# Mask of the first tile added to the scores on TensorE, scheduler priorities by batch, and a last output tile in two column halves, in an attention and gated-MLP kernel

One core of one Trainium2 chip. The metric is the time of one execution in microseconds (us) on the device. Unless it says otherwise, a position is in us from the start of the profiled span, which is some 2 us shorter than the time of the execution.

## The reference

```python
# q, k, v: (4 batches, 8 heads, 768 positions, 64) float32; block = 32; 24 blocks
scores = np.matmul(q, k.transpose(0, 1, 3, 2)) / np.sqrt(64)
mask = (abs(blk_i - blk_j) <= 1) | (first and last block, rows and columns)
mask |= (3 sampled blocks in each block row)
scores = np.where(mask, scores, -1e9)
attn = softmax(scores) ;  x = (attn @ v) as (3072 tokens, 512)
h = x @ w_in                      # w_in: 512 x 2048
out = (h / (1 + np.exp(-beta * h))) @ w_out        # w_out: 2048 x 512
```

## The kernel before

Scores are made transposed (keys on partitions), two heads together, each on 64 rows of the array. ACT takes the exponential of 1024 scores a partition, DVE multiplies it by a 0/1 mask, PE multiplies by the values with one column of ones for the sum, and DVE divides. Four such head pairs give a tile of tokens (256 or 512). For it PE makes 16 hidden pieces, ACT a tanh of each (the gate is written with tanh), DVE the product, PE the output, ACT or DVE the copy, and a DMA stores it.

```python
            def mm(sc=sc, kc0=kc0):
                kX, qX = at(kq)
                for i in range(kn):
                    for hh in range(2):
                        pe.matmul(
                            at(sc)[:, hh, i * n:(i + 1) * n],
                            lhsT=kX[hh * D:(hh + 1) * D, (kc0 + i) * P:(kc0 + i + 1) * P],
                            rhs=qX[hh * D:(hh + 1) * D, q0:q0 + n].rearrange(
                                "d (g c p) -> d c g p", c=CG, p=P),
                            start=True, stop=True)
            def ex(eng, sc=sc, et=et):
                act.activation(out=..., in_=..., func=AF.Exp, bias=0.0, scale=SCALE)
            def mk(eng, et=et, kc0=kc0):
                ...
                dve.tensor_tensor(out=e, in0=e, in1=m, op=ALU.mult)
```

The order of instructions on each engine is made ahead by a list scheduler in the kernel's own Python. All pieces of work are nodes with durations and dependencies. At each step it takes the node with the smallest sum of earliest start and a priority of its kind; the priorities are fitted numbers.

```python
                bias = BIAS[n.kind]
                ...
                key = (n_start + n.dur[e] - min(n.dur.values()) + bias, n.place)
                if best is None or key < best[0]:
                    best = (key, n, e, n_start)
```

The weights come by the DMA queue of POOL in four parts (two of w_in, two of w_out), the first held back until a certain k tile has landed; q, k, v by the queue of SP.

The softmax here doesn't subtract the row's maximum and nothing guards it: scores larger than these inputs give would overflow.

## Time and profile before

| before | |
|---|---|
| time, median (this and its later runs) | 277.1 us (276.2 to 279.0 over all later runs) |
| profiled span | 275.0 us |
| first exponential | 6.86 |
| first hidden matmul of the first (256 wide) tile | 30.18 |
| first hidden matmul of the second (512 wide) tile, "the boundary" | 61.12 |
| last matmul's end, and the tail after it | 270.7, and 4.2 us |

The table is a skeleton of the span: a ramp up to the boundary, a body in which PE has no break, and a tail. The lines behind it are in the prediction. All spans and milestones below are from one profiled execution of each kernel; ratios are from several runs.

### The profile page before, as it was taken

The numbers are of one execution on the slowest core, as the hardware profiler recorded it, in microseconds if no ns is written. First come the engines' busy times: TensorE is split into PE (matmuls) and PEld (weight loads), VectorE is DVE, ScalarE is ACT, GpSimd is POOL, SyncE is SP. The second block draws the span as 40 slices with busy tenths as digits, with TensorE's granted clock in tenths as the row PEclk, the third lists the DMA queues.
The fourth block names the chain that finished last, engine by engine and source line by source line (L and its number), as shares of the span: only waits on it lengthen the run. The fifth ranks groups of instructions, "written<-read, shape, count | busy, mean of one in ns | idle before, by whom it ended". The sixth has DMA issues, their size and how long they took to land.

```text
span 275.0 us, 6172 instructions
## 1 busy us (share of the span) xinstructions
PE 259.7 (94%) x2455; PEld 139.7 (51%) x2455; DVE 209.2 (76%) x416; ACT 217.1 (79%) x284; POOL 32.5 (12%) x53
## 2 busy tenths in 40 slices
PE   6677899969999999999999999999999999999993
PEld 2454674544455464455464444444545644567441
DVE  4789999998797798798988787977787877628000
ACT  3799998998789988789988788987798977529110
POOL 7243000043200112110010111030000000000000
PEclk9999999999999999999999999999999999999999
DMA  6999995599521798796577529490121300020222
GB/s 178 295 267 213 207 205 143 150 265 210 145 49 49 194 165 225 169 220 139 174 190 172 112 61 258 88 224 8 55 62 54 44 12 0 13 86 2 77 76 77
DMA packets 72882, 36.66 MB, mean 133 GB/s; under 512 B 29828, under 2 KB 68756, under 8 KB 72852
## 3 DMA queue, kind: packets, MB, share of 16 engines
q1 hardware_dynamic: 69600, 32.06, 47.3%
q0 software_dynamic: 3136, 4.19, 8.6%
q8 instruction: 19, 0.31, 0.5%
q14 instruction: 11, 0.09, 0.1%
q10 hardware_dynamic: 116, 0.01, 0.0%
HBM read 27.27 MB, written 6.29 MB: 122 GB/s over the span
## 4 chain that ended last, share of the span: by engine, by line
PE 88%; DVE 5%; ACT 2%; DMA 2%; SPq 1%; issue 1%; ACTq 0%; DVEq 0%
PE sc L208 88%; DVE et L208 2%; ACT et L208 2%; DMA st_k<-in_k_dram 2%; DVE xst L208 1%; SPq L477 1%; DVE recip L208 0%; DVE kX L208 0%; DVE s_k L208 0%; DVE xT_sb L208 0%; ACT qX L208 0%; ACT osb L208 0%; SPq L474 0%; DVE s_q L208 0%; DVE qX L208 0%
## 5 line engine op out<-in xcount | busy, mean ns | idle before, releaser
L208 ACT ACTIVATE et<-sc 128x1024 f16<-128x1024 f32 x144 | 136.4, 1045 | 13.9 <-PE sc L208 13.4
L208 DVE TENSOR_TENSOR et<-et,mask 128x1024 f16<-128x1024 f16 x144 | 94.8, 693 | 8.1 <-ACT et L208 8.0
L208 PE MATMUL sc<-w_out_sb,g 128*128 128x512 f16 x384 | 90.0, 379 | 0.0
L208 PE MATMUL sc<-xT_sb,w_in_sb 128*128 128x512 f16 (+1 forms) x448 | 84.3, 349 | 1.1 <-DVE xT_sb L208 1.0
L208 ACT ACTIVATE t_sb<-sc,beta_h_sb 128x512 f16<-128x512 f32 (+1 forms) x112 | 68.2, 649 | 17.1 <-PE sc L208 17.1
L208 DVE SCALAR_TENSOR_TENSOR g<-t_sb,sc 128x512 f16<-128x512 f16 (+1 forms) x112 | 67.6, 611 | 16.0 <-ACT t_sb L208 15.6
L208 PEld LDWEIGHTS <-w_in_sb 128*128 128x128 f16 x448 | 43.8, 98 | 40.7 <-issue 1.5
L208 PEld LDWEIGHTS <-g 128*128 128x128 f16 x384 | 34.6, 98 | 43.2 <-issue 7.5
L208 PE MATMUL sc<-qX,kX 64*128 64x256 f16 (+1 forms) x384 | 44.0, 339 | 4.7 <-ACT qX L208 1.9
L208 PEld LDWEIGHTS <-et 128*128 128x128 f16 x1152 | 39.7, 98 | 9.7 <-issue 6.6
L208 PE MATMUL sc<-va,et 128*128 128x65 f16 x1152 | 42.4, 194 | 1.1 <-ACT et L208 1.0
L208 PEld LDWEIGHTS <-kX 64*128 64x128 f16 x384 | 16.4, 98 | 26.5 <-issue 19.2
L208 ACT ACTIVATE osb<-sc 128x512 f32<-128x512 f32 x18 | 11.0, 608 | 17.9 <-PE sc L208 17.9
L208 DVE TENSOR_TENSOR xst<-sc,recip 128x256 f16<-128x256 f32 x48 | 20.3, 424 | 1.8 <-DVE recip L208 0.2
L497 POOL CAST s_k<-st_k 128x768 f16<-128x768 f32 (+1 forms) x11 | 8.2, 753 | 76.7 <-DMA st_k<-in_k_dram 76.6
L208 DVE RECIPROCAL recip<-sc 128x4 f32<-128x4 f32 x48 | 8.7, 180 | 10.4 <-PE sc L208 8.7
L497 POOL CAST s_q<-st_q 128x768 f16<-128x768 f32 (+2 forms) x11 | 9.0, 821 | 33.4 <-DMA st_q<-in_q_dram 33.0
L497 POOL CAST va<-st_v 128x768 f16<-128x768 f32 x7 | 6.6, 939 | 19.7 <-PE sc L208 15.2
L208 DVE CAST va<-st_v 128x768 f16<-128x768 f32 x9 | 5.0, 558 | 0.9 <-DMA st_v<-in_v_dram 0.9
L208 PE MATMUL sc<-identity,s_k 128*128 128x128 f16 x24 | 3.5, 305 | 2.0 <-DVE s_k L208 1.2
L208 DVE CAST s_k<-st_k 128x768 f16<-128x768 f32 x7 | 3.9, 554 | 1.4 <-issue 0.7
L208 DVE COPY xT_sb<-sc 128x256 f16<-128x256 f16 (+1 forms) x9 | 3.1, 346 | 1.8 <-PE sc L208 1.8
(53 smaller groups left out, 44.6 us busy)
## 6 DMA issues: line engine op xcount, KB each, us to landing
st_v<-in_v_dram SPq DMA_DIRECT2D x16, 384.0 KB, 5.1
out_dram<-osb SPq DMA_DIRECT2D x24, 256.0 KB, 2.2
st_k<-in_k_dram SPq DMA_DIRECT2D x15, 384.0 KB, 4.8
st_q<-in_q_dram SPq DMA_DIRECT2D x12, 384.0 KB, 4.2
w_in_sb<-in_moe_w_in_dram POOLq DMA_DIRECT2D x2, 1024.0 KB, 9.9
w_out_sb<-in_moe_w_out_dram POOLq DMA_DIRECT2D x2, 1024.0 KB, 16.6
st_q<-in_q_dram SPq DMA_DIRECT2D x12, 128.0 KB, 4.6
st_k<-in_k_dram SPq DMA_DIRECT2D x3, 128.0 KB, 2.6
```

The costliest lines, as they stand in the source:

```text
L208: r = f(*a, **kw)
L477: nc.sync.dma_start(out=o[:, g::NG], in_=hg[:, g::NG])
L497: e(out=at(dst)[:, :, :, 0:D] if nm == "v" else by_chunk(dst, lo, hi), in_=src)
```

## The change

The intent: take 12 mask multiplies off DVE in the ramp by adding -30000 to the closed scores on PE before the exponential (two more matmuls of the one-hot block pattern in front of each score pair of the first tile); give each batch its own priorities; let the last output tile end in a shorter copy and store; and let the scheduler's model know that the loading queue has eight lanes. The buffers were newly divided as well.

```diff
-BIAS = {"av": -69, "beta": -455, "cast": 94, "dma": -1239, "ex": 257, "gm": -727, "hp": -468,
+BIAS = {"av": (-653, -382, -588, -2130),
+        "beta": (141, 4011, -951, 12518),
... (25 entries, four numbers each)
+ORDER = "k0a q0 k0b k0c v0 k1 q1 v1 k2 q2 v2 k3 q3 v3 r0 r1 r2 r3"
+N_PEMASK = 4
+GATES = ("k3", None, None, None)
...
+                if e == "SP":
+                    for i in range(n.lanes):
+                        n_start = max(n_start, lane[(n_lane + i) % 8])
-                bias = BIAS[n.kind]
+                bias = BIAS[n.kind][n.part]
...
-                wire[other] += both / RATE[other]
+                wire[other] += both / RATE[e]
...
-    SLOTS = {"st_k": 2, "st_q": 5, "st_v": 5, "s16_k": 4, "s16_q": 2, "set": 4, "va": 4,
-             "et": 13, "xst": 5, "recip": 7, "t_sb": 6, "g": 2, "osb": 3, "sc": 4}
+    SLOTS = {"st_k": 2, "st_q": 3, "st_v": 2, "s16_k": 3, "s16_q": 2, "set": 7, "va": 5,
+             "et": 17, "xst": 6, "recip": 30, "t_sb": 4, "g": 2, "osb": 2, "sc": 4}
... (in the score step)
+                        if by_pe:
+                            r = slice(hh * D, (hh + 1) * D)
+                            pe.matmul(
+                                at(sc)[:, hh, i * n:(i + 1) * n],
+                                lhsT=onehot[r, (kc0 + i) // CG, :],
+                                rhs=shut_qk[r, ...],
+                                start=True, stop=False)
...
-                            start=True, stop=True)
+                            start=not by_pe, stop=True)
... (in the output step)
+            end = t0 + ts * P + P == N_TOK
+            w = D_MODEL // 2 if end else D_MODEL
+            for m0 in range(0, D_MODEL, w):
... (matmuls, copy and store of w columns each)
```

## The prediction

> **What bounds the kernel now.** I read the page from the top: who is busy, and when.
>
> ```profile
> PE 259.7 (94%) x2455; PEld 139.7 (51%) x2455; DVE 209.2 (76%) x416; ACT 217.1 (79%) x284; POOL 32.5 (12%) x53
> PE   6677899969999999999999999999999999999993
> ACT  3799998998789988789988788987798977529110
> ```
>
> PE is the engine, but not in all of the span: the slices (6.9 us each) show it short of 9 in the first five, in the ninth and in the last. The table of stretches (columns: stretch, length, then busy us of PE, PEld, DVE, ACT, POOL, then clock, DMA share, GB/s) says who is full there.
>
> ```profile
> 5.00:10.00 5.00, 3.71 (x30) 2.14 (x29) 2.54 (x7) 3.87 (x6) 2.02 (x5) 1.00 1.05 295
> 20.00:25.00 5.00, 3.62 (x47) 1.83 (x46) 4.73 (x10) 5.00 (x7) 2.76 (x4) 1.00 1.13 215
> 25.00:30.00 5.00, 4.20 (x66) 2.59 (x64) 4.33 (x12) 5.00 (x6) 0.00 (x0) 1.00 1.13 208
> 55.00:60.00 5.00, 3.28 (x66) 2.36 (x63) 4.93 (x11) 5.00 (x6) 1.88 (x3) 1.00 0.96 255
> 150.00:200.00 50.00, 50.00 (x413) 23.93 (x412) 40.77 (x72) 42.20 (x55) 5.96 (x7) 1.00 0.49 119
> ```
>
> From 20 to 60 us ACT is full and DVE nearly; from 61 us on PE is full and ACT has a sixth of its time free. So there are two regimes: to 61 us the exponentials on ACT set the pace, after it PE does. The busy share hides how slow PE is at first; the timeline shows it with equal bundles of 12 score matmuls:
>
> ```profile
> 10.92 1.46 PE L208 MATMUL sc<-qX,kX 64*128 64x256 f16 x12 [0.96 <-ACT qX L208]
> 17.95 0.83 PE L208 MATMUL sc<-qX,kX 64*128 64x256 f16 x12 [0.92 <-ACT qX L208]
> 61.12 5.12 PE L208 MATMUL sc<-xT_sb,w_in_sb 128*128 128x512 f16 x23 [0.58 <-DVE xT_sb L208]
> ```
>
> The last line is the boundary: the first hidden-layer matmul of the second token tile (512 wide). From there to the end the chain of waits has PE in one unbroken piece:
>
> ```profile
> 60.65 0.43 DVE xT_sb L208
> 61.12 209.62 PE sc L208 x1870
> 270.81 0.60 ACT osb L208
> ```
>
> To turn this into a ledger I took the start-to-start distance of matmuls of one kind in the warm part of the trace: 216 ns for 512 columns, 109 for 256, 32 for a value matmul (65 columns), 56 for a transpose; a score pair (two heads, different rows of the array) 216 or 110 together. Times the counts this gives 239.7 us of work, 35.3 below the span. By stretch the difference is 17.8 us in 0 to 30, 1.1 in 30 to 50, 3.4 in 50 to 60, 4.2 in the tail after the last matmul, and some 8 in 61 to 270. The order of instructions has 76 changes between 64-row and 128-row matmuls in that last stretch, so 105 ns a change explains those 8 us.
>
> **What the Trainium skill says.** "TensorE: Matmul & The Clock Gate", Part 1: PE starts at half clock until it has been busy through a whole window of about 3.4 us, 107 against 56 ns for 128 columns. The trace agrees: transposes early are 107 ns apart (median), later ones 56, and the two bundles above are 1.46 and 0.83 us. The same page, Part 3, The mechanism: matmuls on different row groups run together, starting about 4 ns apart. Here the second head starts 3 to 4 ns after the first. The mask matmuls are such pairs, so 48 of them cost 24 single ones. "ScalarE: Activation LUTs", What ACT_TABLE_LOAD costs: 186 ns + 0.833 per element, with 93 ns overlapped back to back; for 1024 elements an estimate of 946 ns. The trace has 144 exponentials in 136.4 us, 947 each. "DMA: Bandwidth & Descriptors", Anatomy of one DMA: some 2 us are fixed per transfer. The output stores land 2.2 us after issue at 256 KB, so halving one can't halve its tail.
>
> **The change, part by part.**
>
> Mask on PE, first tile only. It takes 12 mask multiplies off DVE: 12 x 0.69 = 8.3 us (group of et<-et,mask, 693 ns), in 9 to 19 us. It adds 48 matmuls of 256 columns in 24 pairs: 24 x 0.11 = 2.6 us warm, 24 x 0.24 = 5.8 us cold (12 in 1.46 us). It also takes DVE out of the path from exponential to values, and lets the values of head pair 3, whose exponentials were done by about 21.5 us but whose values ran only at 27.15, run earlier. Its price at the start: a PSUM-to-SBUF ACTIVATE of 384 columns (estimate 0.5 us between the 0.37 of 256 columns and the 0.65 of 512) now sits on ACT before the first exponential, and cold mask pairs precede the first scores. The first exponential, at 6.86 us, I put at 7.4.
>
> Priorities. The order of the two builds shows what they do. ACT reaches its first 512-wide tanh after 41 exponentials instead of 45, and the first 256-wide tanh after 18 instead of 23: less attention ahead, hidden layer earlier. Hidden work costs PE far more per ACT time (a 512-wide hidden step: 4 x 216 ns of PE for one 0.69 us tanh, and as much PE again for the output layer) than attention (216 ns of scores and 8 x 32 of values for 947 ns), so this moves PE's full regime forward. I add up ACT between its first exponential and its first 512-wide tanh:
> - before: 45 x 0.947 = 42.6; 16 narrow tanh x 0.41 = 6.6; 2 output copies 1.2; one token copy 0.6; three narrow and one wide q copy 1.8: 52.8 us. The stretch is 62.19 - 6.86 = 55.3, so 2.5 us are gaps.
> - after: 41 x 0.947 = 38.8; tanh 6.6; output copies 1.2; one 768-wide k copy (estimate 0.9) and one q copy 0.4: 47.9 us, plus the same 2.5 of gaps.
> So the first wide tanh comes at 7.4 + 50.4 = 57.8 instead of 62.2, and the first wide hidden matmul, 1.1 us ahead of it as now, at 56.7 instead of 61.1: 4.4 us gained.
>
> The weights allow it, just. Both halves of w_in land 9.9 us after issue (15.37 and 20.25), at 25.3 and 30.1 us; before, the hidden layer starts at 30.18, so only the second half was used on arrival. The new order runs the first 32 hidden matmuls, scores, then the rest, which fits the two arrivals. The two halves of w_out release their waiters at 35.3 and 40.9, and the new order meets them with output pieces of 4 matmuls with attention between.
>
> After the boundary. PE's remaining work by the same costs is 202.4 us against 201.7, with 78 row changes against 76: 0.9 us given back. ACT is tighter in the first wide hidden tile and what follows: between the first wide matmul and that of the next tile it gets 31 exponentials, 16 wide tanh (0.69) and 3 output copies, 42 us, and PE some 43.5. ACT is 97% full there against 89% before (26 exponentials); I charge 0.5 us for waits.
>
> Last output tile in halves. The last ACT copy has 256 columns instead of 512: 0.60 to an estimated 0.38. The store has 128 KB instead of 256: perhaps 0.3 us less of the 2.2. Matmul time stays (32 x 109 against 16 x 216). Sum 0.5 us.
>
> DMA lanes in the model. They cost nothing on the chip; they make the planned order of loads closer to what the queue does. Fewer staging buffers (q 5 to 3, v 5 to 2) pay for more exponential buffers (13 to 17). I give it 0.
>
> Sum: 275.0 - 4.4 + 0.9 + 0.5 - 0.5 = 271.5 us of span, 3.5 less. On the median of 277.07 that is 273.6. I take 273.0: the gaps (2.5 us) are probably smaller in the new order too, since DVE has 8.3 us less to do exactly where they lie (ACT waited there for copies of q and k that stood behind mask multiplies), and the author tuned for that.
>
> **Rivals.** (1) The ramp gives nothing: cold mask matmuls delay the second head pair's scores, since in the new PE order the values of the first pair stand ahead of them. If those 24 matmuls run cold (1.53 us, as at 13.19 now) ACT idles up to 2 us near 11. For it: the 1.46 us bundles. Against it: PE is busy without break from 5 us on, so its clock may rise sooner. It would make 275. (2) ACT stays the bound beyond the boundary because it has less done ahead, 41 exponentials against 45, and the gain is handed back in 57 to 100 us. For it: 97%. Against it: by the second wide tile 72 exponentials are done against 71. It would make 275 to 276. (3) Loads arrive late with fewer staging buffers, and PE waits in the middle. For it: the load queue already stood from 41.9 to 52.2 us behind stores and transposes. Against it: PE has no loss at all in 65 to 250 beyond row changes. It would make 274 to 278. (4) The clock rises early and DVE's relief closes the gaps: the boundary moves to 54 to 55 us and the time to 271.
>
> **Range and chances.** The sum rests on one large term, 4.4 us, uncertain by some 2 us each way (start of the first exponential, gaps), and on no new stall later. So 273.0, with 270.2 to 275.7 for 8 in 10. Faster by over 2% needs less than 271.5, which takes rival 4: 0.28. Slower by over 2% would need a broken prefetch: 0.03.
>
> **What would show it.** Right: the first wide hidden matmul at 55.5 to 58 us; the stretch 55 to 60 with PE near 5.0; first exponential at 7.2 to 7.7; the first narrow hidden matmul near 25.5 (w_in) rather than 30.2; PE unbroken after the boundary, some 214 us from it to the end; the last ACT copy near 0.38 us. Wrong: ACT gaps of over 1 us near 11, PE waits for et or DMA after 60, or a boundary still at 60.

## The result, and the profile after

| | before | after |
|---|---|---|
| time, median of 4 runs | 277.11 us (276.81 to 277.69) | 272.70 us (272.37 to 273.64) |
| profiled span | 275.0 | 270.5 |
| first exponential | 6.86 | 7.17 |
| values of the fourth head pair | 27.15 | 21.67 |
| first narrow hidden matmul | 30.18 | 25.37 |
| the boundary | 61.12 | 55.88 |
| last matmul's end | 270.73 | 266.97 |
| tail | 4.22 | 3.50 |

The ratio is 0.9844, with a 95% interval of 0.9815 to 0.9873. A ratio here is the mean time of one kernel's fast runs over that of the other's of the same rounds, so not quite the ratio of the medians.

From the page of the kernel after, the engines' busy us with their shares, and PE and ACT in 40 slices:

```profile
PE 260.1 (96%) x2519; PEld 141.5 (52%) x2519; DVE 194.1 (72%) x397; ACT 216.8 (80%) x289; POOL 37.3 (14%) x58
PE   6988999999999999999999999999999999999994
ACT  4898999799988989979978878987898788695111
```

Besides the first slice and the last, PE is short of 9 in slices 3 and 4 only, where it was so in 2 to 5 and in 9. DVE has 15 us less to do: 7.4 of them are mask multiplies, and six output copies (4.1) have gone to ACT, some casts to POOL. The stretches of the kernel after (same columns as in the prediction):

```profile
5.00:10.00 5.00, 4.76 (x44) 3.05 (x44) 2.18 (x6) 4.11 (x8) 2.13 (x4) 1.00 1.12 305
20.00:25.00 5.00, 4.04 (x68) 2.36 (x65) 3.85 (x11) 3.88 (x6) 1.12 (x2) 1.00 1.14 219
25.00:30.00 5.00, 4.52 (x41) 3.52 (x41) 4.84 (x14) 5.00 (x12) 0.00 (x0) 1.00 1.12 210
55.00:60.00 5.00, 4.54 (x27) 1.85 (x26) 4.77 (x7) 4.98 (x7) 3.62 (x4) 1.00 1.34 309
150.00:200.00 50.00, 50.00 (x413) 23.93 (x411) 36.95 (x66) 42.54 (x55) 6.35 (x8) 1.00 0.46 116
```

The stretch 55 to 60, in which PE had 3.28 us of 5, is now 4.54: the body has moved into it. ACT has given back time in 20 to 25 (3.88 for 5.00). It is a wait of 1.12 us for scores whose second half of q came late. The timeline (start, length, engine, line, operation, tiles and shapes, then the idle time ahead and who ended it) around the start of the hidden layer and around the boundary:

```profile
25.34 0.35 PEld L244 LDWEIGHTS <-w_in_sb 128*128 128x128 f16 x4 [0.64 <-DMA w_in_sb<-in_moe_w_in_dram]
25.37 0.60 PE L244 MATMUL sc<-xT_sb,w_in_sb 128*128 128x256 f16 x4 [0.50 <-DVE xT_sb L244]
31.06 1.05 PE L244 MATMUL sc<-xT_sb,w_in_sb 128*128 128x256 f16 x8 [0.29 <-DMA w_in_sb<-in_moe_w_in_dram]
55.88 3.63 PE L244 MATMUL sc<-xT_sb,w_in_sb 128*128 128x512 f16 x16
59.97 2.32 PE L244 MATMUL sc<-xT_sb,w_in_sb 128*128 128x512 f16 x10 [0.46 <-DVE g L244]
```

The first narrow hidden matmul waits for two things at once: its weights (PEld is released by the landing of w_in's first half) and its tokens (PE is released by DVE's copy of xT_sb). Before, only the second bound:

```profile
30.18 4.00 PE L208 MATMUL sc<-xT_sb,w_in_sb 128*128 128x256 f16 x33 [0.45 <-DVE xT_sb L208]
```

The chain of waits of the kernel after (start, length, what) now begins with another part of the same load, the second half of w_in, which landed at 31.01 and for which PE waited 0.29 us:

```profile
18.58 12.43 DMA w_in_sb<-in_moe_w_in_dram
31.06 3.55 PE sc L244 x32
...
59.97 207.02 PE sc L244 x1882
267.00 0.38 ACT osb L244
```

Its last piece of PE has no break for 207 us, as before (209.6), and the copy behind it takes 0.38 us, not 0.60. So the 4.5 us of span are -5.2 at the boundary, +1.5 from there to the last matmul (211.1 for 209.6), and -0.7 in the tail.

### The profile page after: what moved, and what is told of

Its sections match the earlier page's. It is cut to its first block, busy times and chain, and to the rows that moved or that the text cites. A ratio compares the mean times of both kernels' runs of the same rounds, so it can differ in the third digit from the quotient of the medians.

```text
span 270.5 us, 6288 instructions
## 1 busy us (share of the span) xinstructions
PE 260.1 (96%) x2519; PEld 141.5 (52%) x2519; DVE 194.1 (72%) x397; ACT 216.8 (80%) x289; POOL 37.3 (14%) x58
## 4 chain that ended last, share of the span: by engine, by line
PE 82%; DMA 5%; DVE 3%; ACT 2%; issue 0%
PE sc L244 82%; DMA w_in_sb<-in_moe_w_in_dram 5%; DVE et L244 2%; ACT et L244 2%; DVE xT_sb L244 0%; DVE g L244 0%; DVE xst L244 0%; ACT osb L244 0%; DVE recip L244 0%
## 5 line engine op out<-in xcount | busy, mean ns | idle before, releaser
L244 DVE TENSOR_TENSOR et<-et,mask 128x1024 f16<-128x1024 f16 x132 | 87.4, 704 | 6.4 <-ACT et L244 6.2
L244 PE MATMUL sc<-w_out_sb,g 128*128 128x512 f16 (+1 forms) x400 | 90.3, 371 | 0.0
L244 PE MATMUL sc<-xT_sb,w_in_sb 128*128 128x512 f16 (+1 forms) x448 | 86.8, 349 | 1.3 <-DVE xT_sb L244 0.5
L244 DVE SCALAR_TENSOR_TENSOR g<-t_sb,sc 128x512 f16<-128x512 f16 (+1 forms) x112 | 64.4, 607 | 15.7 <-ACT t_sb L244 15.4
L244 ACT ACTIVATE t_sb<-sc,beta_h_sb 128x512 f16<-128x512 f32 (+1 forms) x112 | 66.0, 637 | 11.7 <-PE sc L244 7.3
L244 ACT ACTIVATE osb<-sc 128x512 f32<-128x512 f32 (+1 forms) x25 | 14.8, 590 | 19.4 <-PE sc L244 18.7
L565 POOL CAST va<-st_v 128x768 f16<-128x768 f32 x12 | 10.5, 873 | 64.9 <-DMA st_v<-in_v_dram 64.1
L565 POOL CAST s_q<-st_q 128x768 f16<-128x768 f32 (+1 forms) x11 | 8.9, 811 | 12.0 <-DVE g L244 5.4
L244 PE MATMUL sc<-shut_qk,onehot 64*128 64x256 f16 x48 | 6.8, 306 | 0.4 <-ACT et L244 0.4
L244 DVE CAST s_q<-st_q 128x512 f16<-128x512 f32 (+2 forms) x9 | 3.7, 407 | 1.5 <-DMA st_q<-in_q_dram 1.5
```

Source lines behind the costliest of these rows:

```text
L244: r = f(*a, **kw)
L565: e(out=at(dst)[:, :, :, 0:D] if nm == "v" else by_chunk(dst, lo, hi), in_=src)
```

## The experiments

All twelve kernels give the right result. They ran in four groups, each on one chip and beside runs of the kernel before on it: e1, e2, e6, e7; then e3, e4, e5, e9; then e0, e12, e13 (five rounds each); then e14 (three rounds). Two ways of ablation are used, and the difference turned out to matter: some rerun the scheduler on a changed input, so that the whole order moves; some keep the order of the changed kernel and alter one thing in it. Where the profile of a kernel is quoted, it is of one execution.

### The last tile

**e1**: before, with the output step of the change (two halves in the last tile). Apart from the last tile the order is that of before.

```diff
+            end = t0 + ts * P + P == N_TOK
+            w = D_MODEL // 2 if end else D_MODEL
+            for m0 in range(0, D_MODEL, w):
```

> The kernel before with only the last output tile in two halves; all other instructions keep their order. My theory: only the end changes. The last output copy takes 0.38 us instead of 0.60 and the last store ends sooner, so the span falls by 0.5 to 0.8 us, from 275.0 to about 274.3 (ratio 0.997 to 0.998). Rival, the fixed part of a store hides it: only the copy's 0.22 us show, span 274.8 (0.999). Either way the first wide hidden matmul stays at 61.1 us.

**e2**: the changed kernel with its last tile whole.

```diff
-            w = D_MODEL // 2 if end else D_MODEL
+            w = D_MODEL
```

> The changed kernel with its last output tile whole again; nothing else moves. My theory: the halves are worth the 0.74 us by which the stretch from the last matmul to the end is shorter (4.27 against 3.53 us), so the span becomes 271.0 to 271.3 and the ratio to before 0.987. Rival, the halves are worth nothing: 270.5, ratio 0.984.

**e12**: the changed kernel with the last tile cut at 384 and 128 columns.

```diff
-            for m0 in range(0, D_MODEL, w):
+            for m0, w in ((0, 384), (384, 128)) if end else ((0, D_MODEL),):
```

> The changed kernel with its last output tile cut at 384 and 128 columns instead of 256 and 256. Theory (after the last matmul only the last part's copy and store remain): the last copy falls from 0.38 to about 0.28 us and its store of 64 KB lands some 0.1 us sooner, tail 3.3 to 3.4 us against 3.53, so 0.1 to 0.3 us less in all, ratio 0.983 to 0.986, within the spread of the times. Rival: the first part's larger store (192 KB), issued shortly before, keeps the queue, and the tail is 3.5 or more.

Measured: e1 0.9979 [0.9942, 1.0017], 276.46 us; e2 0.9844 [0.9803, 0.9884], 273.16 us (0.987 was expected); e12 0.9837 [0.9802, 0.9872], 272.32 us. The last copies in the timelines of e1 and of e12:

```profile
271.26 0.38 ACT L208 ACTIVATE osb<-sc 128x256 f32<-128x256 f32 x1 [1.31 <-PE sc L208]
```

```profile
266.61 0.49 ACT L244 ACTIVATE osb<-sc 128x384 f32<-128x384 f32 x1 [2.00 <-PE sc L244]
267.45 0.28 ACT L244 ACTIVATE osb<-sc 128x128 f32<-128x128 f32 x1 [0.36 <-PE sc L244]
```

From last matmul to end of span: 4.2 us before, 3.5 in e1 and after, 4.0 in e2, 3.1 in e12 (the expectation of e2 has 4.27 and 3.53, from rounded spans). In the traces the halves are worth 0.5 to 0.7 us, and the cut at 384 another 0.4, a little more than I had expected. In the times none of it is resolved: the interval of e1 includes 1, and e2 has the changed kernel's ratio. The times of one kernel differ by more than 1 us between runs; where from is the last experiments' subject.

### The mask on PE, with the order kept

**e6**: the changed kernel's order on ACT, SP, POOL and PE; the mask matmuls are taken out, and 12 mask multiplies go into DVE's order behind their exponentials.

```diff
-                        if by_pe:
+                        if False:
...
-                            start=not by_pe, stop=True)
+                            start=True, stop=True)
+    for e, f, et in late:                 # after the scheduler has run
+        n = Node("mk", "DVE", 0, 0, f)
+        seq.insert(first_after(e, et), n)
```

> The changed kernel in its own order on PE, ACT, SP and POOL, but without the mask matmuls: the 12 masks of the first tile are multiplied on DVE again, each at the first place in DVE's queue at which its exponential is planned to be done. My theory: the order lives off DVE's relief. DVE is busy 5.9 of 10 us in 10 to 20 us, 8.3 us more do not fit without delay, and the values of the first tile wait for their masks: first narrow hidden matmul 1 to 4 us later than 25.4, first wide one at 57 to 60 instead of 55.9, ratio 0.988 to 0.996. Rival, the order alone makes the gain and the mask matmuls only cost PE 2.6 us and the first exponential 0.4 us: same as the changed kernel or faster, ratio 0.980 to 0.985.

**e7**: the mask matmuls doubled (the closed scores get -60000, with the same result).

```diff
+                            for again in range(2):
                               pe.matmul(
...
-                                start=True, stop=False)
+                                start=again == 0, stop=False)
```

> The changed kernel with each mask matmul issued twice (48 more, in 24 pairs, at the same places). My theory: they lie beside ACT, which sets the pace of the first tile, so most of the 2.6 to 5 us added to PE is hidden; the first exponential comes 0.4 us later (two more cold pairs ahead of it) and the time grows by 0.4 to 1.2 us, ratio 0.986 to 0.989. Rival, PE is on the path there: 3 us or more longer, ratio 0.995 or above.

Measured: e6 0.9908 [0.9879, 0.9937], 274.75 us; e7 0.9903 [0.9873, 0.9932], 274.68 us. DVE (third busy column) in 15 to 25 us, first in the kernel after, then in e6:

```profile
15.00:20.00 5.00, 3.86 (x71) 2.88 (x66) 2.87 (x10) 5.00 (x6) 3.11 (x4) 1.00 1.10 233
20.00:25.00 5.00, 4.04 (x68) 2.36 (x65) 3.85 (x11) 3.88 (x6) 1.12 (x2) 1.00 1.14 219
```

```profile
15.00:20.00 5.00, 3.24 (x56) 2.32 (x56) 5.00 (x12) 4.15 (x6) 4.52 (x5) 1.00 1.19 258
20.00:25.00 5.00, 3.74 (x69) 2.55 (x66) 5.00 (x13) 4.46 (x6) 0.00 (x0) 1.00 1.12 210
```

With the multiplies DVE is full for those 10 us, and everything that stands behind it is late: the tokens of the first tile (first hidden matmul at 27.57 for 25.37) and with them the boundary (57.62 for 55.88). The two places in e6:

```profile
27.57 0.60 PE L244 MATMUL sc<-xT_sb,w_in_sb 128*128 128x256 f16 x4 [0.91 <-DVE xT_sb L244]
57.62 3.63 PE L244 MATMUL sc<-xT_sb,w_in_sb 128*128 128x512 f16 x16
```

PE waits in 15 to 30 us for DVE's copies of q, k and the tokens. So in this order the mask on PE is worth 1.7 us at the boundary, and the times agree (e6's median is 1.6 us above that of e2, the same order but for the last tile, in the same rounds). The other 3.5 of the 5.2 us come with the order itself, its new buffers included (61.12 to 57.62, e6 having no mask on PE). Not separated from DVE's relief is the clock: the trace's first record of a full clock is at 9.5 us in the kernel after, 14.6 in e6 and 16.6 before. In the ten profiles with the mask on PE it comes at 8.5 to 14.4 us, in the four without at 14.6 to 19.3.

e7 costs more than I had expected for 24 pairs: the first exponential is 0.62 us later, the first hidden matmul 1.11, the boundary 0.80, but the next wide tile 2.1 us later (102.17 for 100.08). The second loss is at the boundary itself. Timelines there, after and then e7:

```profile
55.58 3.74 DVE L244 TENSOR_TENSOR et<-et,mask 128x1024 f16<-128x1024 f16 x4
56.21 1.34 POOL L565 CAST va<-st_v 128x768 f16<-128x768 f32 x1 [0.50 <-DMA st_v<-in_v_dram]
```

```profile
56.37 5.04 DVE L244 TENSOR_TENSOR et<-et,mask 128x1024 f16<-128x1024 f16 x4
58.79 0.85 POOL L565 CAST va<-st_v 128x768 f16<-128x768 f32 x1 [0.37 <-DMA st_v<-in_v_dram]
```

Four multiplies take 5.04 us in e7, 3.74 after, and 2.5 at their usual 0.62 from one to the next; POOL casts run beside them: three in the kernel after (up to 1.34 us, 0.83 alone), five in e7 (0.83 to 1.07). The Trainium skill, "SBUF — State Buffer", Who interferes with whom, says that a VectorE instruction with two SBUF inputs contends with a GpSimd instruction that reads SBUF. The direction fits both traces. No run isolates it, and casts and multiplies overlap in the records, so I claim no more than that this place is sensitive to when POOL's casts fall.

### The parts, with the scheduler run again

**e3**: the change without the mask on PE. **e4**: the change with the priorities of before. **e5**: before, with the mask on PE alone. **e9**: the change with the second part of q of the first head pair loaded one place earlier, meant to close ACT's gap of 1.12 us.

```diff
-N_PEMASK = 4                                   # e3
+N_PEMASK = 0
+BIAS = {"av": -69, ... of before}              # e4
+BIAS = {k: (v,) * 4 for k, v in BIAS.items()}
+N_PEMASK = 4                                   # e5, in before, with the code of the mask matmuls
-ORDER = "... k3 q3 v3 r0 r1 r2 r3"             # e9
+ORDER = "... k3 q3 r0 v3 r1 r2 r3"
```

> The changed kernel with no tile masked on PE; the scheduler is free to make another order (36 exponentials before the first wide tanh and 23 before the first narrow one, 45 between the first wide hidden matmul and that of the next tile). My theory: the mask on PE is what lets these priorities pay. The first narrow hidden matmul comes at 28 to 31 us as in the kernel before, and ACT has 45 exponentials and 16 wide tanh, 54 us, to do in the first wide hidden tile, for which PE needs 48, so that PE waits there. Ratio 0.989 to 0.999. Rival, the priorities make the gain alone: 0.985 or less.

> The changed kernel with the priorities of before, the same in each batch. The order has 43 exponentials before the first wide tanh instead of 41, 19 before the first narrow one, and three token copies on ACT. By my ledger that is 2 x 0.95 + 3 x 0.4 = 3 us more on ACT before the boundary, which lies at 58 to 60 us: ratio 0.992 to 0.998. Rival, the mask on PE makes the gain and the priorities none: 0.984 to 0.987.

> The kernel before with the mask of the first tile on PE and nothing else (its priorities, buffers and loads). The order has 18 exponentials before the first narrow tanh instead of 23, but still 45 before the first wide one. My theory: the boundary is set by ACT's sum, which is that of before plus 0.5 us for making the mask operand: first narrow hidden matmul at 25 to 27 us, first wide one still at 60 to 62, ratio 0.997 to 1.004. Rival, DVE's relief alone shortens the ramp: boundary at 57 to 58, ratio 0.986 to 0.990.

> The changed kernel with the second part of the first q loaded before the last v of the first four pairs. In the changed kernel ACT waits 1.12 us near 20 us for scores that need this q (landed at 18.6). My theory: the gap closes, but the new order puts 42 exponentials before the first wide tanh instead of 41, so the two cancel: ratio 0.982 to 0.987. Rival, the gap was on the path and nothing comes back: 0.980 or less.

| | ratio and interval | median | first hidden | boundary | next wide tile |
|---|---|---|---|---|---|
| e3 | 1.0900 [1.0862, 1.0939] | 302.42 | 37.34 | 68.57 | 130.26 |
| e4 | 0.9986 [0.9967, 1.0005] | 277.23 | 27.40 | 60.50 | 101.92 |
| e5 (one slow run left out) | 1.0182 [1.0149, 1.0215] | 282.22 | 27.64 | 62.37 | 108.78 |
| e9 | 1.0419 [1.0379, 1.0460] | 288.85 | 25.57 | 58.87 | 105.91 |

Three of four missed what I had expected, by 1.4% (e5) to 9% (e3), and e4 missed narrowly. None is the change less one part. In each the scheduler makes another order, and with priorities fitted to another problem it makes a poor one. In e3 PE waits 4.4 us for a q cast in 20 to 36 (from the waits of PE, in total, times, longest), its clock is halved for most of 30 to 40 (seventh number), and PE is idle after the boundary too; e9 has such a wait at 140 to 180. The lines, e3 twice, then e9:

```profile
PE sc L244 <- DVE s_q L244: 4.4, 1, 4.4
30.00:40.00 10.00, 6.83 (x52) 4.35 (x53) 7.58 (x18) 3.90 (x7) 1.34 (x2) 0.51 0.92 161
```

```profile
PE sc L244 <- DVE va L244: 3.4, 1, 3.4
```

What follows: the parts don't add up. Everything but the new priorities gives nothing (e4), the mask alone costs 1.8% under the old ones (e5), and the new ones without the mask cost 9% (e3). I conclude that the gain belongs to the order that was fitted for exactly this program; which of its features make the 3.5 us no run isolates. A build without a run belongs here: with the lane term alone taken out of the scheduler's model, the program comes out identical on all five engines. So that term by itself does nothing in this kernel.

### The early clock, and the spread of the times

e2 is the changed kernel up to its last tile, and yet its first 24 value matmuls took longer in the trace than those of the kernel after, the second line here, by the half clock of PE:

```profile
10.72 1.53 PE L244 MATMUL sc<-va,et 128*128 128x65 f16 x24
```

```profile
9.68 1.20 PE L244 MATMUL sc<-va,et 128*128 128x65 f16 x24
```

Its score matmuls ran at half rate until 14.4 us. I took this for the source of the spread, and ran the changed kernel again (**e0**, no edit) beside a version whose early idle time is filled (**e13**).

> The changed kernel, unaltered, to have its spread and its early clock beside the next two. Expected 0.984 to 0.987 of the time before, medians 272.4 to 273.4. My theory of the ramp (the same program gets its full clock at 9 to 11 us in some runs and near 14 in others) says that single times spread over at least 1.5 us and that the profiled run shows the first bundle of 24 values either near 1.2 us or near 1.5. The rival (the late clock in the run with a whole last tile came from that kernel, not from chance) says spread below 0.8 us and the bundle near 1.2 again.

```diff
+                if lo == 0 and (x, nm) in ((0, "q"), (1, "k")):
+                    for _ in range(4 if x else 3):
+                        pe.matmul(at(tb)[:, 0:256 if x else 128], lhsT=warm[:, 0:P],
+                                  rhs=warm[:, 0:256 if x else 128], start=True, stop=True)
```

> The changed kernel with seven dummy matmuls more (three of 128 columns before the first q transposes, four of 256 before the k transposes of the second head pair), placed where PE waits in its first 11 us; the order is otherwise the same. If it is PE's idle time there that delays the clock, the profile shows the value bundle near 1.2 us or less, the boundary at or below 56.0, the single times spread less than those of the unaltered kernel, and the ratio is 0.980 to 0.984. If the phase of the clock is set by something else than PE's work, the dummies only stand in the way: boundary 56 to 57, ratio 0.984 to 0.988, spread as before.

Measured: e0 0.9861 [0.9829, 0.9893], 273.10 us (272.45 to 274.47); e13 0.9862 [0.9819, 0.9905], 273.35 us (271.75 to 276.41, of which the highest is a slow run and left out of the ratio). The boundary of e13 is as expected (55.57), but the value bundle took 1.33 us where 1.2 or less was expected, since the full clock came at 11.4 us, later than in the kernel after (9.5); and its times are neither better nor closer together. And the profile of e0 contradicts me: its values ran early and fast (9.60, 0.99 us), its thirteenth exponential was the earliest of all (20.85), and its boundary was the latest, 57.39. The time was lost later. Timeline and stretches of e0:

```profile
25.68 0.61 PE L244 MATMUL sc<-xT_sb,w_in_sb 128*128 128x256 f16 x4 [1.31 <-DMA w_in_sb<-in_moe_w_in_dram]
26.35 4.89 PE L244 MATMUL sc<-xT_sb,w_in_sb 128*128 128x256 f16 x28
25.00:26.00 1.00, 0.33 (x3) 0.31 (x4) 1.00 (x3) 1.00 (x2) 0.00 (x0) 1.00 1.15 222
27.00:28.00 1.00, 1.00 (x6) 0.71 (x5) 0.59 (x2) 0.47 (x1) 0.00 (x0) 0.50 1.13 218
```

The same 28 hidden matmuls took 3.26 us in the kernel after. Here PE had waited 1.31 us for w_in, the granted clock fell to 0.50 from about 26.6 to 30, and they took 4.89: 1.63 us lost. With the 0.31 us by which they began late this covers the 1.51 that its boundary is late. There are five profiles of the changed order up to its last tile (after, e0, e2, e12, e13). In four of them the boundary comes 30.4 to 30.6 us behind the first narrow hidden matmul; in e0 it is 31.7. From this came the last theory: what binds is the start of the hidden layer, with the weights' landing and the tokens abreast and no slack in either.

**e14**: the first half of w_in is issued behind a cast on POOL, with all other orders kept.

```diff
+    w = [n for n in seq if n.kind == "weights"][:3]
+    for n in w[:2]:
+        seq.remove(n)
+    i = seq.index(w[2])
+    seq[i:i] = w[:2]
```

> The changed kernel with the first half of w_in issued behind the cast of v of the second head pair, so at about 19 us instead of 15.2 and just ahead of the second half; every other engine and queue keeps its order. The new theory, from the six profiles of this order so far: the boundary is the first narrow hidden matmul plus 30.0 to 30.6 us, and that start is bound by the landing of w_in's first half (25.3 us) and by the token copies behind the values (25.1 to 25.4) at once, with no slack in either. Then w_in lands at 27 to 28.5, the boundary moves by as much to 57.5 to 59, and the ratio rises from 0.984 to 0.990 to 0.995. Rival, the ledger of the prediction taken alone (the exponentials on ACT from the first one on set the boundary, and the weights have slack): boundary below 56.5 and ratio 0.984 to 0.987. A third way: the loads of q land earlier without the weights beside them, the ACT gap of 1.12 us near 20.2 closes, and half of the loss comes back: boundary 56.8 to 57.4.

Measured: 1.0028 [0.9993, 1.0064], 277.65 us: the whole gain is gone. Timeline and stretches of e14:

```profile
28.42 1.01 PE L244 MATMUL sc<-xT_sb,w_in_sb 128*128 128x256 f16 x4 [3.66 <-DMA w_in_sb<-in_moe_w_in_dram]
29.66 4.90 PE L244 MATMUL sc<-xT_sb,w_in_sb 128*128 128x256 f16 x28
31.00:32.00 1.00, 1.00 (x6) 0.67 (x5) 0.42 (x1) 0.62 (x2) 0.00 (x0) 0.50 1.10 202
```

The weights landed at 28.3, as expected, the first hidden matmul came 3.1 us late, but the boundary 4.9 us late (60.75; 57.5 to 59 was expected). The difference is the clock again: 0.50 from about 26.3 to 33.1. The second half of w_in landed 2.6 us later too, but PE had no wait for it. So a w_in that is 3 us late isn't hidden, and it is charged twice, first as the wait and then as a half-rate hidden layer behind which ACT waits (in e0 four gaps of 0.38 us between 27 and 30). ACT's gap near 20.2 did shrink (0.21 for 1.12 us) with the q loads undisturbed, and it bought nothing: the values of the fourth head pair came at 21.57 for 21.67.

That w_in is what always binds, these runs do not show. Its first half landed 0.81 us after the last token copy in e0, but 0.03 us before it in the kernel after, 0.12 in e12, 0.39 in e13 and 1.06 in e2:

```profile
26.19 0.60 PE L244 MATMUL sc<-xT_sb,w_in_sb 128*128 128x256 f16 x4 [0.50 <-DVE xT_sb L244]
```

That is e2, where the tokens alone bind. In these four the boundary follows the first exponential (7.00, 7.17, 7.36 and 7.37 us; boundary 55.57, 55.88, 56.33 and 56.62), as the prediction's ledger would have it.

Does this make the spread? Of 27 fast executions of the changed order (after, e0, e2, e12, e13), 21 have a mean granted clock of 0.997 or more and a mean time of 272.7 us; the 6 others have 0.992 to 0.994 and 274.4. (The 3.4 us at half clock of e0 take 0.006 off the mean.) These 1.7 us are the size of e0's loss. But only e0's profile shows where its clock fell. In e1 and e6 there are runs of 0.992 to 0.994 that are no slower than their fellows, so a low mean clock alone is no proof. Of the cause of the spread I hold shown one instance, and the rest likely.

## Why the prediction was right

The time is 272.7 for a predicted 273.0. By its own steps:

- **First exponential**, 7.4: it is 7.17, and 6.87 to 7.37 over five profiles of this order.
- **DVE's relief**, "in 9 to 19 us": misread. The 12 multiplies of the first tile ran from 8.98 to 27.47 us before; the last began at 26.79, and all but the first four value matmuls of the fourth pair waited for it (27.53). So DVE did stand in the way of these values, and its relief is spread over a longer stretch.
- **ACT's ledger**: 50.4 us from the first exponential to the first wide tanh; measured 7.17 to 57.44, 50.3. It was right. The 2.5 us of gaps that it carried over left 2.4 (as idle time of ACT in the traces, 4.2 and 4.1), so the guess that "the gaps (2.5 us) are probably smaller in the new order too" was wrong. The 0.6 us taken off for it, 273.6 to 273.0, came near the result by luck; other terms made the difference.
- **The boundary**, 56.7: it is 55.88. Of the 0.8 us, 0.36 are the earlier tanh (57.44 for 57.8), and 0.46 are the lead of matmul over tanh, 1.56 us where I had kept 1.1.
- **After the boundary**, +0.9 for PE's work and row changes and +0.5 for waits: +1.5 together. PE's idle time there is 0.46 us in all, the wait at 59.97 (0.01 before), so 1.0 is work and row changes.
- **The tail**, -0.5: it is -0.72 in the trace, under-sized, and not resolved in the times. The copy gave 0.22 as predicted, the store 0.36 for a predicted 0.3: the last store landed 2.21 us after issue at 256 KB before, 1.85 at 128 KB after, 1.60 at 64 KB in e12.
- **Lanes in the model**, 0: right in the strict sense that the program is the same without that term.

The rivals. (1), cold mask matmuls and an ACT gap near 11 us, does occur: ACT waits 0.84 us there in the kernel after and 1.71 in e2, where the values ran cold (1.53 us, as the rival had it). It is not hidden: e2's first narrow hidden matmul is 0.82 us and its boundary 0.74 us later than those of the kernel after. But it costs that, and not the whole gain. (2), ACT as the bound beyond the boundary, fell: PE has 5.00 of 5 us in 60 to 65. Of the 5.2 us only 3.3 are left at the next wide tile (100.08 for 103.40), but in between PE has more scores to make (84 matmuls for 68) and waits only 0.46 us. (3) as written, loads late in the middle, did not occur. (4) was half right: the clock did rise early (9.5 us for 16.6), but the gaps did not close, and the boundary of 55.9 is not its 54 to 55; in those five profiles it lies anywhere from 55.6 to 57.4.

What the prediction did not see is the price when the weights are late. It wrote "The weights allow it, just.", which holds in four of the five profiles, by 0.03 to 1.06 us; in the fifth they came 0.81 us after the tokens, and PE lost its clock as well. Nor did it separate the order from the mask. With the order kept, e6 gives 1.7 us to the mask and 3.5 to the order, at the boundary.

As to a better version: e12's tail is 0.4 us shorter than that of the kernel after, and its median of 272.32 is the lowest of all, but its interval overlaps with e0's of the same rounds (0.9802 to 0.9872, and 0.9829 to 0.9893), so it is not shown to beat the changed kernel. An order that always has a few tenths of slack in w_in was not found, and stays open.

## What to carry to other kernels

In a kernel with a fitted order, ablate inside the order that runs; rerunning the scheduler without a part measures the scheduler, here up to 9% on the wrong side. Add up the engine that paces the ramp between two milestones of the trace, and then ask what else arrives at the second milestone, since the gain ends where the next arrival stands. A wait of PE just ahead of dense work is charged twice if the clock falls in it.

## What the Trainium skill lacked or had wrong

- "TensorE: Matmul & The Clock Gate", Why this matters for your kernels: its advice is to avoid idle gaps of PE of over some 3 us. In e0 the longest gap was 1.31 us, in a stretch where PE was busy for 0.70, 0.48, 0.36 and 0.33 us of four successive microseconds, and the granted clock fell to 0.50 for about 3.4 us, 1.63 us lost on 28 matmuls. So it fell without a gap of that length. The same page's section "A second HAM failure mode" (HAM is its name for what watches PE and sets the clock) does tell of short idle pieces, but without a size. Here the records of the clock lie whole multiples of 3.41 us apart within a trace. In the last such piece before the fall in e0 (23.17 to 26.59) PE was busy for 1.58 of 3.42 us; in the piece of the kernel after, e2, e12 and e13 that precedes or holds the start of the hidden layer it was busy for 2.1 to 2.5 us, and all kept their clock. No threshold is claimed: in e9 a piece with 1.51 us (65.90 to 69.31) kept it too.
- The same page, Part 1, gives the moment of the first full clock, for matmuls back to back, a run-to-run spread of 500 ns either way, and in its note calls the count of cold matmuls run-variable. Five profiles of one and the same opening, with gaps in PE's work (e13's has seven dummies more), have it between 8.5 us (e12) and 14.4 us (e2), so several microseconds. That the ramp matters for less than 1% of a span agrees: the boundaries of these two are 0.3 us apart.
- The same page, Part 4, says that the full clock doesn't engage for transposes on PE. Here 128-column transposes run 107 ns apart early and 56 ns apart later, so they do run at the full clock once it is there. Whether they help to raise it no run shows.
- "SBUF — State Buffer", Who interferes with whom, gives no size for two-input multiplies beside casts. Here four two-input multiplies took 3.74 and 5.04 us beside POOL casts, for 2.5 at their usual pace.
- No page says that a trace may hold no record of the granted clock before its first rise (9.5 us in the kernel after, 16.6 before), so that a table can print 1.00 there while matmuls run at half rate (5 to 10 us here, score pairs 213 ns apart for 109 later). The distance between matmuls and the time of the first record show the cold start, and agree.
